# A transformer block on one core: one down tile moved from the attention loop into the tail's norm, wider spacing of one chunk's gate and up blocks, transposed tiles copied ahead of due work, and a reordered prologue

## The chip, the cores and the metric

The kernel runs on one core of a Trainium2 chip. A core has a matrix engine (TensorE, PE in the profile, with PEld for its weight loads), a vector engine (VectorE, DVE), a scalar engine that evaluates functions (ScalarE, ACT), a general engine (GpSimd, POOL) and a queue that issues transfers (SyncE, SP). Each works through its own list of instructions in order and waits on semaphores for the others. TensorE writes to PSUM; the other data is in SBUF. The metric is device time in microseconds, the median of several runs.

## The reference: what is computed

One transformer block, pre-norm, for 2048 rows of 512 features in bf16: 32 attention heads of 16 features, then a gated feed-forward layer of width 1792.

```python
def _A_ref(x, wqkv, wo):                      # S=2048, D=512, H=32, Dh=16
    qkv = (x @ wqkv).reshape(B, S, 3, H, Dh).transpose(2, 0, 3, 1, 4)
    q, k, v = qkv[0], qkv[1], qkv[2]
    scores = jnp.einsum("bhqd,bhkd->bhqk", q, k) * (Dh ** -0.5)
    p = _softmax(scores, axis=-1)
    o = jnp.einsum("bhqk,bhkd->bhqd", p, v)
    return o.transpose(0, 2, 1, 3).reshape(B, S, D) @ wo

def _B_ref(x, w_gate, w_up, w_down):          # F=1792
    g = jnp.einsum("bsd,df->bsf", x, w_gate)
    u = jnp.einsum("bsd,df->bsf", x, w_up)
    return jnp.einsum("bsf,fd->bsd", _sigmoid(g) * u, w_down)

h = x + _A_ref(_layernorm(x), wqkv, wo)
h2 = h + _B_ref(_layernorm(h), w_gate, w_up, w_down)
```

Inputs are normal times 0.05. The largest piece of work is 32 x 2048 x 2048 exponentials.

## The kernel before

**Prologue (L264 to L475).** Rows are loaded in tiles of 128. Per pair of tiles `u`, `stats(u)` computes mean and variance on VectorE (ScalarE for one pair), `apply(u)` normalizes, and `trans(u)` transposes on TensorE and copies the result to SBUF on ScalarE (L341). As soon as 512 rows are there, `k_mm(n)` computes their keys for the first heads, `square(n)` squares them for a bound on the scores, and `k_copy(n)` copies them to SBUF (L361) and issues a transfer that spreads them (`k_spread`, L221). `norm_part_of` and `norm_half` (L383, matmul L387) sum the squares, and `k_max` (L179) takes the maxima. From them comes the bound `bnd` (L466), which the scores need so that no exponential overflows. `v_prod` and `v_cast` make the values of tiles 0 and 1. At the end GpSimd copies one element of `bnd` (L472, which makes it wait for the bound) and then clears buffers (L473, L529, L1051). While the prologue runs, `pm_tile()` gives one of six PSUM tiles. `ps_misc` is a pool with a single PSUM tile, and `acc` another single one.

**The attention loop (L1057 to L1072).** The 2048 queries are cut into chunks 0, 1, 2 of 512 rows and chunks 3 and 4 of 256. A unit is one chunk, one group of four heads, one tile of keys and one head. Three units make a step; there are 683 steps. Step `i` writes its scores with TensorE into one of two PSUM buffers of three parts of 512 columns (L879), and ScalarE takes the exponential of all three (L890, 1.45 us). In every fourth step (`i % 4 == 0`, up to step 680, and some more in `twice`) the third part's exponential is left to VectorE as a polynomial: L909 reads PSUM at once, L912 and L915 follow one step later, L918 two, L922 three. The probabilities are multiplied with the values some steps later (`emit_pv`, L961, into `acc`), and at the end of a head group `emit_norm` copies `acc` (L935) and takes the row sums through DRAM and back to get their reciprocals (L938 to L950, on the SP queue); `scale` multiplies (L942) into `OT`.

**Fill work.** All other work of the loop is one generator, `filler`. It yields the cost of each matmul, and `emit_fill(i)`, called once per step, takes as much from it as `rate(i)` allows. A yield of `("at", n)` makes it wait for the next step whose number modulo 4 is `n` (its phase), `("gap", n)` for some steps, and `("from", n)` for step `n`. In the loop `pm_tile()` gives the one tile of `ps_misc`, so each piece of fill work waits until the one before it has been read out of PSUM.

**Order inside a step.** A step emits, in this order: scores, exponential, PV, what is due at this step (`due`: polynomial pieces, reciprocals, scalings, normalizations put there by `later`), and the fill work. Only in a step in which a head group's first PV unit falls is the fill emitted ahead of that unit. Since each engine works in order, this is also the order on VectorE.

**Feed-forward of a finished chunk (`ffn_tasks(c)`).** For each 128-row tile, `ffn_wo` (chunks 0, 1) or `ffn_wo_tight` (chunks 2, 3) runs eight projection matmuls (L598), adds x and normalizes (`wo_ln`, L607 and the norm's lines, the normalization itself two steps later), and then `hn_transpose` transposes (L162) and copies (L163). `ffn_up` runs gate blocks and up blocks alternately: eight matmuls of 256 columns or four of 512 (L622), the gate followed by a tanh on ScalarE (L627), the up block by a product on VectorE (L635). `ffn_down` runs 14 matmuls per tile (L638) and adds the residual (L643). Chunk 3's feed-forward runs during chunk 4's attention, and `wo_early` begins chunk 4's projection.

**Tail (`ffn_last`).** After the last exponential chunk 4's two tiles are finished alone: projection, statistics (L785, L795), normalized tile 0 on ScalarE (L798) and tile 1 on VectorE (L800), transposes (L791), copies (L792), gate and up, down (L823), output. `spin` issues matmuls whose result nobody reads (L253): six while the norm is computed, two after each transpose.

Of the kernel before, what the change touches and what calls it, by code (L numbers as in the profile page):

```python
# [19 lines left out]
def kernel(  # L20
# [243 lines left out]
    def prologue(pro):  # L264
# [156 lines left out]
        norm_part_of(0)  # L421
        k_chunk(1)
        stats(6)
        apply(5)
        trans(5)
        norm_mm_to(acc[:], sqs["q"])
        v0 = v_prod(0, pm_tile())
# [30 lines left out]
        half_copy(1)  # L458
        k_spread(ku, 0, slice(3 * QC, S), nc.sync)
        pn3 = ps_misc.tile([P, 512], FP32, name="pm")  # L460
        norm_half(pn3, 7)
        k_max(pn3[:, 0:QC // 2], km2[:, 2:3])
        v_cast(1, v_prod(1, ps_misc.tile([P, 512], FP32, name="pm")))
        m2 = k_most()
# [149 lines left out]

    def hn_transpose(tt, hn, copy=None):
        transpose4(hnT[:, :, tt * P:(tt + 1) * P], hn, copy)

# [29 lines left out]
    def ffn_wo(c):  # L647
        for tt, t in enumerate(tiles_of(c)):
            xr = x_load(t)
            yield ("at", 3)  # L650
            ps = pm_tile()
            for g in range(NG):
                if g == NG // 2:
                    yield ("at", 1)
                yield 1
                wo_mm(ps, c, tt, g)
            hn = wo_ln(ps, xr, tt)
            yield ("gap", 1)
            yield ("at", 1)
            yield 1  # L660
            hn_transpose(tt, hn)

    def ffn_wo_tight(c):
        turn = None
        for tt, t in enumerate(tiles_of(c)):
            xr = x_load(t)
            yield ("at", 3)
            ps = pm_tile()
            for g in range(NG):
                if g == NG // 2:  # L670
                    yield ("at", 0)
                yield 1
                wo_mm(ps, c, tt, g)
            hn = wo_ln(ps, xr, tt)
            if turn:
                yield ("at", 1)
                yield 1
                hn_transpose(*turn)
            turn = (tt, hn)
        yield ("gap", 1)  # L680
        yield ("at", 1)
        yield 1
        hn_transpose(*turn)

    def ffn_up(c):
        w = CHUNKS[c][1]
        at = cycle((3, 1) if c + 2 < NC else (3, 0, 1))
        for fs in blocks_of(w):
# [15 lines left out]
    def ffn_down(c, tight):  # L704
        at = 0
        for tt, t in enumerate(tiles_of(c)):
            for f in range(FC):
# [23 lines left out]
    def wo_early(c):  # L731
        early["x"] = [x_load(t) for t in tiles_of(c)]
        early[0] = pm_tile()
        for g in range(NG - 1):
            if g == NG - 2:
                yield ("from", NS - 4)
            yield 1
            wo_mm(early[0], c, 0, g)

    def ffn_last(c):  # L740
# [35 lines left out]
        for tt in range(n):  # L776
            wo(tt, NG - 1, NG)
        spin(acc, wo_pad[:, 0, :], 6)
        mv = small.tile([P, n, nc.vector.BN_AGGR_DIM], FP32, name="mvl")
# [25 lines left out]
        for tt in range(n):  # L805
            nc.vector.tensor_copy(out=h_sb[:, tt, :], in_=pss[tt][:])
        for fs in blocks_of(w):
# [10 lines left out]
        for tt, t in enumerate(ts):  # L818
            for cols in ((0, D),) if tt < n - 1 else ((0, D // 2), (D // 2, D)):
                cs = slice(*cols)  # L820
                psd = pm_tile()
                for f in range(FC):
                    nc.tensor.matmul(psd[:, cs], lhsT=hT[:, f, tt * P:(tt + 1) * P], rhs=wd[:, f, cs],  # L823
                                     start=(f == 0), stop=(f == FC - 1))
                ob = pmh["work"].tile([P, D], BF16, name="ob", tag="xn")
                nc.vector.scalar_tensor_tensor(out=ob[:, cs], in0=psd[:, cs], scalar=0.5, in1=h_sb[:, tt, cs],
                                               op0=ALU.mult, op1=ALU.add)
# [145 lines left out]
    fl = filler()  # L973
    state = {"wait": 0, "debt": 0.0, "done": False, "next": 0, "rate": None}

# [63 lines left out]
    with tc.manual_schedule():  # L1039
# [17 lines left out]
        for i in range(NS + LAG):  # L1057
# [7 lines left out]
            for u in us:  # L1065
                if early_fill and u[2] == 0:
                    emit_fill(i)
                emit_pv(*u[:3], i)
            for fn in due.pop(i, []):
                fn()  # L1070
# [39 lines left out]
```

## Time and profile before

| what | value |
|---|---|
| median of 3 runs | 959.14 us (958.26 to 960.2) |
| the profiled execution's own time | 958.45 us |
| its span, first to last instruction | 956.6 us |
| ScalarE busy | 898.2 us, 94% of the span |
| TensorE busy | 839.0 us, 88% |
| VectorE busy | 783.3 us, 82% |
| GpSimd busy | 40.0 us, 4% |
| first exponential starts, last one ends | 29.82 us, 926.60 us |
| granted TensorE clock | 1.0 of full speed |

The profile is one execution. Busy is the time in which an engine works on at least one instruction; shares are averages over stages with different limits. A row of the timeline gives the start, the duration, engine, line, operation, output<-inputs, the count of merged instructions, and in brackets how long the engine had been idle and what released it. A row of the waits gives who waited for whom, the microseconds in total, how many times, and the longest. TensorE's matmuls overlap: one of 512 columns takes about 0.38 us from start to end, but several together take less than their sum. Spans on GpSimd are rough.

### The profile page before, as it was taken

Reading aid. Unit: us, or ns where it says so; the run is one execution under the profiler, and the core shown is the slowest. Engines: PE = TensorE matmul, PEld = TensorE weight load, DVE = VectorE, ACT = ScalarE, POOL = GpSimd, SP = SyncE. Lnnn points to the kernel's source line nnn. Section 1 sums busy time; section 2 is a strip of 40 time slices with the busy share of each in tenths; the row PEclk is TensorE's granted clock in tenths of the full one; section 3 lists DMA queues with packets and bytes.
Section 4 is the critical chain, followed back from the end, with each engine's and each line's share of the span. In section 5 each row is a group of like instructions: output and inputs, shape, how many; then the busy total and the mean of one; then the engine's idle time right before and its main releaser. Section 6 shows DMA issues by size and latency. Waiting matters only on the chain.

```text
span 956.6 us, 17273 instructions
## 1 busy us (share of the span) xinstructions
PE 839.0 (88%) x6433; PEld 336.9 (35%) x6433; DVE 783.3 (82%) x1413; ACT 898.2 (94%) x778; POOL 40.0 (4%) x56
## 2 busy tenths in 40 slices
PE   5998888888788999998788999988788999998998
PEld 3322222222222322222222323222355555455656
DVE  7589988888788888899888888898898788777653
ACT  6889999999999999999999999999998999999872
POOL 5600000000000000000000000000000000000000
PEclk9999999999999999999999999999999999999999
DMA  5102350000003000000010000000010000110010
GB/s 161 24 2 56 115 117 16 16 16 14 16 14 103 15 16 17 20 24 23 4 26 27 16 17 16 19 9 27 16 31 23 17 10 15 27 32 16 10 35 12
DMA packets 37645, 28.45 MB, mean 30 GB/s; under 512 B 17788, under 2 KB 32920, under 8 KB 37560
## 3 DMA queue, kind: packets, MB, share of 16 engines
q1 hardware_dynamic: 37416, 27.22, 10.8%
q8 instruction: 50, 0.82, 0.4%
q14 instruction: 35, 0.29, 0.1%
q10 hardware_dynamic: 144, 0.13, 0.0%
HBM read 20.31 MB, written 2.61 MB: 24 GB/s over the span
## 4 chain that ended last, share of the span: by engine, by line
PE 45%; ACT 24%; DVE 22%; issue 6%; DMA 2%; SPq 1%; POOL 0%; ACTq 0%; DVEq 0%
PE pss L879 21%; ACT pt L890 13%; PE acc L961 8%; PE pm L622 7%; ACT stg L890 4%; ACT wd L890 4%; DVE stg L909 2%; PE pm L638 2%; ACT QTu L890 2%; PE pm L598 2%; PE pm L171 2%; DVE y L918 2%; DVE pt L922 2%; DVE reg L912 1%; DVE reg L635 1%
## 5 line engine op out<-in xcount | busy, mean ns | idle before, releaser
L879 PE MATMUL pss<-QB,KT 128*128 128x512 bf16 (+3 forms) x2554 | 476.0, 337 | 80.7 <-ACT pt L890 40.2
L890 ACT ACTIVATE pt<-pss 128x1536 bf16<-128x1536 f32 (+1 forms) x392 | 502.2, 1366 | 14.0 <-PE pss L879 9.5
L879 PEld LDWEIGHTS <-KT 64*128 64x128 bf16 (+1 forms) x2554 | 179.3, 95 | 340.5 <-issue 232.8
L890 ACT ACTIVATE stg<-pss 128x1536 bf16<-128x1536 f32 (+1 forms) x140 | 183.4, 1361 | 5.0 <-PE pss L879 3.8
L909 DVE TENSOR_SCALAR stg<-pss 128x512 int32<-128x512 f32 x123 | 84.8, 690 | 68.1 <-PE pss L879 59.9
L961 PE MATMUL acc<-pt,Vaug 128*17 128x512 bf16 (+1 forms) x1471 | 112.5, 338 | 2.3 <-DVE pt L922 1.1
L890 ACT ACTIVATE wd<-pss 128x1536 bf16<-128x1536 f32 (+1 forms) x80 | 103.9, 1391 | 1.9 <-PE pss L879 1.4
L890 ACT ACTIVATE QTu<-pss 128x1024 bf16<-128x1024 f32 (+1 forms) x71 | 95.9, 1350 | 1.7 <-PE pss L879 1.3
L915 DVE SCALAR_TENSOR_TENSOR y<-reg 128x512 f32<-128x512 f32 x123 | 85.2, 692 | 4.2
L918 DVE SCALAR_TENSOR_TENSOR y<-y,reg 128x512 f32<-128x512 f32 x123 | 84.3, 685 | 1.1
L961 PEld LDWEIGHTS <-Vaug 128*17 128x17 bf16 x2560 | 49.2, 89 | 94.7 <-issue 80.3
L622 PE MATMUL pm<-reg,reg 128*128 128x512 bf16 (+1 forms) x280 | 57.9, 337 | 7.9 <-DVE reg L635 7.6
L622 PE MATMUL pm<-reg,wu 128*128 128x512 bf16 (+1 forms) x280 | 58.1, 338 | 1.4 <-ACT sg L627 1.1
L638 PE MATMUL pm<-wd,reg 128*128 128x512 bf16 x196 | 55.6, 382 | 1.9 <-DVE ob L643 1.9
L912 DVE TENSOR_SCALAR reg<-stg 128x512 int32<-128x512 int32 x123 | 52.0, 422 | 1.8
L961 PE MATMUL acc<-stg,Vaug 128*17 128x256 bf16 (+1 forms) x564 | 50.6, 326 | 0.3 <-DVE stg L922 0.2
L635 DVE SCALAR_TENSOR_TENSOR reg<-sg,pm 128x512 bf16<-128x512 f32 x56 | 38.2, 683 | 14.2 <-PE pm L622 13.8
L922 DVE SCALAR_TENSOR_TENSOR pt<-y,stg 128x512 bf16<-128x512 f32 x70 | 48.0, 686 | 2.0
L152 POOL TENSOR_TENSOR rs<-ve,pw_neg 128x1 f32<-128x1 f32 x16 | 11.8, 735 | 877.1 <-DVE ve L150 870.5
L627 ACT ACTIVATE sg<-pm 128x512 f32<-128x512 f32 x56 | 36.5, 651 | 10.4 <-PE pm L622 9.9
L909 DVE TENSOR_SCALAR wd<-pss 128x512 int32<-128x512 f32 x45 | 31.0, 689 | 17.9 <-PE pss L879 16.5
L171 PE MATMUL pm<-reg 128*128 128x512 bf16 x124 | 38.3, 398 | 1.8 <-DVE stg L526 0.7
(151 smaller groups left out, 715.8 us busy)
## 6 DMA issues: line engine op xcount, KB each, us to landing
rb_all<-rd SPq DMA_DIRECT2D x96, 64.0 KB
xr<-in_A_x_dram SPq DMA_DIRECT2D x16, 128.0 KB
out_dram<-ob SPq DMA_DIRECT2D x15, 128.0 KB
rb_all<-rd SPq DMA_DIRECT2D x60, 32.0 KB
reg<-in_A_x_dram SPq DMA_DIRECT2D x7, 256.0 KB
KT<-stg SPq DMA_DIRECT2D x7, 256.0 KB
reg<-in_B_w_gate_dram SPq DMA_DIRECT2D x4, 448.0 KB
wu<-in_B_w_up_dram SPq DMA_DIRECT2D x4, 448.0 KB
```

Of the source, the lines that this page charges most:

```text
L171: nc.tensor.matmul(ps[:], lhsT=wqkv_sb[:, c, w0:w0 + P], rhs=xnT[:, c, n * QC:(n + 1) * QC], start=(c == 0), stop=(c == DC - 1))
L622: nc.tensor.matmul(ps[:, i * w:(i + 1) * w], lhsT=wt[:, c, f * P:(f + 1) * P], rhs=hnT[:, c, 0:w], start=(c == 0), stop=(c == DC - 1))
L635: nc.vector.scalar_tensor_tensor(out=out, in0=a, scalar=1.0, in1=b, op0=ALU.add, op1=ALU.mult)
L638: nc.tensor.matmul(ps[:], lhsT=hT[:, f, tt * P:(tt + 1) * P], rhs=wd[:, f, :], start=(f == 0), stop=(f == FC - 1))
L879: nc.tensor.matmul(pss[:, ui, h * w:(h + 1) * w], lhsT=KT[rows, g, kt * P:(kt + 1) * P], rhs=QB[n_qg % 2][rows, j, 0:w], start=True, stop= ...
L890: ex = nc.scalar.activation(out=pt[:, 0:na, :], in_=pss[:, 0:na, :], func=ACT.Exp, scale=DH ** -0.5 / QS)
L909: return nc.vector.tensor_scalar(out=e_bits, in0=src, scalar1=ONE_BITS, scalar2=0.0, op0=ALU.add, op1=ALU.max)
L912: nc.vector.tensor_scalar(out=e_man, in0=e_bits, scalar1=0x7FFFFF, scalar2=-0x40800000, op0=ALU.bitwise_and, op1=ALU.bitwise_or)
L915: nc.vector.scalar_tensor_tensor(out=e_pol, in0=m, scalar=PA, in1=m, op0=ALU.add, op1=ALU.mult)
L918: nc.vector.scalar_tensor_tensor(out=e_pol, in0=e_pol, scalar=PB, in1=e_man.bitcast(FP32), op0=ALU.add, op1=ALU.mult)
L922: nc.vector.scalar_tensor_tensor(out=dst, in0=e_pol, scalar=PC, in1=e_bits.bitcast(FP32), op0=ALU.add, op1=ALU.mult)
L961: nc.tensor.matmul(acc[32 * j:32 * j + VW, 0:w], lhsT=Vaug[:, kt, 4 * g + j, :], rhs=p[:, h * w:(h + 1) * w], start=(kt == 0), stop=(kt == ...
```

## The change

- `ffn_down(3)` leaves out its last tile. `ffn_last` runs that tile's 14 matmuls in place of the six `spin` matmuls in the norm, and its `down_out` after the copies of the two residual tiles. Those copies go to slots `n + tt` of `h_sb`, since the left-out tile's residual is still in slot 1.
- `ffn_up(3)` places its blocks at phases 3, 1, 3, 0, 1 in turn; before, at 3, 0, 1.
- `wo_early` holds its last matmul (group 6) behind the loop by three yields instead of one.
- A flag `state["turn"]` is set before a tile's transposes. In the step in which the fill may go on, the fill is then emitted ahead of what is due, so that the copy of the transposed tile stands on VectorE ahead of the polynomial pieces and scalings of that step. `hn_transpose` clears the flag.
- In the prologue the copy of key chunk 1 (`k_copy(1)`) is issued after `trans(5)`. The value product of tile 1 goes into `acc`, two of its matmuls ahead of `norm_half(7)` and two behind it; before, it used the single tile of `ps_misc` after `k_max` had released it.

```diff
@@ prologue
-        k_chunk(1)
+        ps1 = k_mm(1)
+        square(1, ps1[:])
         stats(6)
         apply(5)
         trans(5)
+        k_copy(1, ps1)
         norm_mm_to(acc[:], sqs["q"])
...
+        for c in range(2):
+            v_mm(acc, 1, c)
         pn3 = ps_misc.tile([P, 512], FP32, name="pm")
         norm_half(pn3, 7)
         k_max(pn3[:, 0:QC // 2], km2[:, 2:3])
-        v_cast(1, v_prod(1, ps_misc.tile([P, 512], FP32, name="pm")))
+        for c in range(2, DC):
+            v_mm(acc, 1, c)
+        v_cast(1, acc)
@@ hn_transpose
+        state["turn"] = False
         transpose4(hnT[:, :, tt * P:(tt + 1) * P], hn, copy)
@@ ffn_wo, and the same before the transposes in ffn_wo_tight
             yield ("gap", 1)
+            state["turn"] = True
             yield ("at", 1)
@@ ffn_up
-        at = cycle((3, 1) if c + 2 < NC else (3, 0, 1))
+        at = cycle((3, 1) if c + 2 < NC else (3, 1, 3, 0, 1))
@@ ffn_down
-        for tt, t in enumerate(tiles_of(c)):
+        for tt, t in enumerate(tiles_of(c)[:None if c < NC - 2 else -1]):
@@ wo_early
             if g == NG - 2:
-                yield ("from", NS - 4)
+                for _ in range(3):
+                    yield ("from", NS + LAG)
@@ ffn_last
-        spin(acc, wo_pad[:, 0, :], 6)
+        psd = pm_tile()
+        for f in range(FC):
+            down_mm(psd, f, len(tiles_of(c - 1)) - 1)
...
         for tt in range(n):
-            nc.vector.tensor_copy(out=h_sb[:, tt, :], in_=pss[tt][:])
+            nc.vector.tensor_copy(out=h_sb[:, n + tt, :], in_=pss[tt][:])
+        down_out(psd, tiles_of(c - 1)[-1], len(tiles_of(c - 1)) - 1)
...
-                nc.vector.scalar_tensor_tensor(out=ob[:, cs], in0=psd[:, cs], scalar=0.5, in1=h_sb[:, tt, cs],
+                nc.vector.scalar_tensor_tensor(out=ob[:, cs], in0=psd[:, cs], scalar=0.5, in1=h_sb[:, n + tt, cs],
@@ the loop, between a step's PV and its due work
+            if state["turn"] and i == state["wait"] and not early_fill:
+                emit_fill(i)
+                early_fill = True
             for fn in due.pop(i, []):
                 fn()
```

## The prediction

> **What bounds the kernel now.** I read the busy times first, then ScalarE's waits stretch by stretch, then the chain and the timeline where those waits are long.
>
> ```profile
> PE 839.0 (88%) x6433; PEld 336.9 (35%) x6433; DVE 783.3 (82%) x1413; ACT 898.2 (94%) x778; POOL 40.0 (4%) x56
> ```
>
> ScalarE (ACT) is busy 94% of the span. From the first exponential (L890, 29.82 us) to the end of the last (926.60 us) it goes from step to step almost without a hole, and its work in that stretch is not changed. So the loop gets shorter by the ScalarE idle time that goes, the start by the time at which the first exponentials can run, and the end by the chain behind the last one. ScalarE's waits from 870 to 930 us (chunk 3's gate, up and down work), then from 733 to 800 us (chunk 2's gate and up work):
>
> ```profile
> ACT pt L890 <- PE pss L879: 2.1, 5, 0.8
> ACT stg L890 <- PE pss L879: 1.5, 4, 0.8
> ACT QTu L890 <- PE pss L879: 0.8, 1, 0.8
> ACT sg L627 <- PE pm L622: 0.4, 1, 0.4
> ...
> ACT stg L890 <- PE pss L879: 0.3, 1, 0.3
> ACT sg L627 <- PE pm L622: 0.2, 1, 0.2
> ```
>
> Here 4.8 us are lost in 60, there 0.5 us in 67. Chunk 2 puts its blocks two steps apart (phases 3, 1), chunk 3 at phases 3, 0, 1, so that two of three follow in adjacent steps. The timeline shows what that does: an up block cannot start before the tanh (L627) has read the one shared PSUM tile, the next scores stand behind the block, and the exponential starts 0.81 us late.
>
> ```profile
> 900.06 0.59 ACT L627 ACTIVATE sg<-pm 128x512 f32<-128x512 f32 x1
> 900.70 1.03 PE L622 MATMUL pm<-reg,wu 128*128 128x256 bf16 x8 [0.45 <-ACT sg L627]
> 902.37 5.29 ACT L890 ACTIVATE pt<-pss 128x1536 bf16<-128x1536 f32 x4 [0.81 <-PE pss L879]
> ```
>
> In chunk 2's norm a transposed tile's copy (L163) stands on VectorE behind the polynomial exponential (L912, L915) and holds the PSUM tile that the next output-projection matmuls want:
>
> ```profile
> 722.59 0.42 DVE L163 COPY reg<-pm 128x512 bf16<-128x512 bf16 x1
> 723.06 1.02 PE L598 MATMUL pm<-wo_pad,OT 128*128 128x512 bf16 x4 [1.01 <-DVE reg L163]
> 725.49 1.02 ACT L890 ACTIVATE pt<-pss 128x1024 bf16<-128x1024 f32 x1 [1.42 <-PE pss L879]
> ```
>
> In the tail's norm TensorE runs six filler matmuls and then waits for the normalized tile:
>
> ```profile
> 930.69 1.46 PE L253 MATMUL acc<-wo_pad,ident_bf 128*128 128x512 bf16 x6
> 933.66 0.40 PE L791 MATMUL pm<-ident_bf,xn 128*128 128x128 bf16 x4 [1.51 <-ACT xn L798]
> ```
>
> And in the prologue:
>
> ```profile
> 20.33 0.62 ACT L361 CAST stg<-pm 128x512 bf16<-128x512 f32 x1
> 21.92 1.02 PE L171 MATMUL pm<-reg 128*128 128x512 bf16 x4 [0.39 <-ACT reg L341]
> 27.38 1.02 PE L166 MATMUL pm<-reg 128*128 128x512 bf16 x4 [0.52 <-DVE km L179]
> 40.62 3.54 POOL L529 MEMSET KT<- 128x2048 bf16 x2
> 43.13 1.31 DVE L912 TENSOR_SCALAR reg<-wd 128x512 int32<-128x512 int32 x1
> ```
>
> **The change, part by part.**
>
> *Blocks of chunk 3 wider, one down tile out of the loop.* Seven gate and seven up blocks, first at step 647. Now they stand at 647, 648, 649, 651 and so on, the last at 664: nine neighbours in adjacent steps. Afterwards they stand at 647, 649, 651, 652, 653, 655, 657, 659, 660, 661, 663, 665, 667, 668: five. The idle time by kind, from ScalarE's holes now: gate then up across phases 3 to 0 is 0.81, 0.81, 0.81; gate then up across 0 to 1 is 0.38, 0.38; up then gate across 3 to 0 is 0.33, 0.35; up then gate across 0 to 1 is 0.43 and 0. Sum 4.30 us. The five that remain are two of the first kind (1.62), one of the second (0.38), one of the third (0.34), one of the fourth (0.21, the mean): 2.55 us. The eight now separated cost what chunk 2's do, 0.5 us in 27 blocks, so 0.15. The down work has holes of 0.13, 0.17, 0.48 and 0.17 (0.95 us) in ten stops; 0.48 is the second tile waiting for the first one's result (L643). Five stops (steps 671 to 676) remain: 0.30. Together 5.25 now, 3.00 after: **-2.25 us**. The ends: -0.65 if the block waits only move, -5.25 if all holes close.
>
> *The tail.* Fourteen matmuls of 512 columns take the place of six fillers. The final down work gives their pitch: 14 of 512 and 28 of 256 columns in 6.24 us is 0.223 each. From 930.69 to the transposes at 933.66 there are 2.97 us; 14 need 3.1. The first transposes slip about 0.1 us, but the second ones (934.38) wait for the other normalized tile, and the gate blocks for its copy: **+0.05 us**, ends 0 and +3.7 (0.379 for one alone and 0.097 for its weight load, as the rows of that final down work, L823, have them, with nothing overlapped: 6.7). The new result (L643, 0.69 us) follows the two copies that end at 936.44 on VectorE, so it ends at 937.13; the first product (L635) starts at 937.33: covered by the two blocks that TensorE runs until then. Should that cover go, 0.7 us at most. Its output transfer has over fifteen microseconds to the end.
>
> *Last projection matmuls.* Group 6 of the early tile stays behind the last PV matmuls as now, at nothing: 926.79 is set by the last exponential. On SP the kept tile's output and two x loads (0.42 and 0.93 us of issue) now come ahead of the last reciprocal's transfers. That reciprocal (921.04) waits 1.65 us for sums whose issue started at 919.39, and the three issues fit into that; the output that stands ahead of those sums now (0.45 us) is gone. The scaled group is ready at 926.33 and wanted at 927.12: 0.8 us of cover, at nothing; 1 us if it is used up.
>
> *Copies ahead of what falls due.* Fourteen copies, each ahead of L912 and L915 (1.1 us) and, in some steps, the scaling (L942). Only two were waited for: 1.01 and 0.18 us. The long one: the copy could run at 721.18 instead of 722.59, the projection matmuls at 722.05, but the sixteen PV matmuls behind them want the accumulator's copy (L935), which still ends at 723.33. They start at 723.38, not 724.01: 0.63. With 0.18 for the other, **-0.8 us**; ends -1.2 and 0. The price: VectorE stands still until the transposes are done. By their ends against the preceding instruction's end that is about 0.3 us at three tiles and under 0.1 at two, in stages where ScalarE has no hole: nothing. Behind each waiting copy stand L912 and L915, with PV five steps off.
>
> *Prologue order.* K copy 1 (L361) moves behind the transposed tile's copy (L341). The chain runs through both, 0.48 us of it in L361. TensorE could start chunk 2's K at 21.46: 0.45 us for all that follows. K copy 1's own transfer waits on SP anyway, behind eight query issues that end at 23.64. The value product of tile 1 in `acc` lets two matmuls run before the norm (L387) and spares the wait of 0.52; its copy also leaves before the first exponential. The bounds (L466) would be ready at 27.77, the first exponential at 28.77: 1.05 us earlier. But GpSimd's nine memsets start with the bounds and move by 0.45 only, their last from 42.37 to 41.92, its end from 44.16 to 43.71. L912, 0.42 us elsewhere, took 1.31 beside it and ended 0.28 after it. From there VectorE runs without a hole to the value copy that releases TensorE at 47.88, and the exponential at 49.53. So what arrives is **-0.45 us**; ends 0 and -1.05.
>
> The SBUF — State Buffer page of the Trainium skill, section "Who interferes with whom", has the rule behind that row: VectorE in a two-port mode and GpSimd share a port pair, whoever issues first holds it for its whole instruction, and the other blocks. By it L912, coming at 42.1, waits for the memset that started at 41.9: -0.45; without it -1.05 would stand.
>
> **Sum:** -2.25 + 0.05 - 0.8 - 0.45 = -3.45 us against the profiled execution's 958.45 (span 956.6 and 1.85 around it): 955.0. The median of the runs is 959.14, 0.69 above the profiled one, so I forecast 955.7 for it.
>
> **The rivals.**
> - *GpSimd's memset is not in the way.* L912 would come only some 0.15 us after the memset's start, and GpSimd's spans are rough; a little earlier, and it slips in. Then -1.05 in place of -0.45: 955.1.
> - *The block waits only move.* TensorE's other work per step stays, and a hole closed at one step may open at the next. For it: step 657's up-then-gate has no hole, step 649's has 0.43, so the kinds are not constant. Against: three holes of 0.81 within 2 ns. Then -0.65 in place of -2.25: 957.3.
> - *The copies win nothing*, because PV or the next norm sets step 540: 956.5.
> - *Slower: the tail's down tile is not covered.* If its matmuls and weight loads do not overlap, +3.7, and the time is 959.3 (with the copies' gain gone too it would be over 960). It decides from 3.5 us over the hole, 0.46 us a matmul. Against it stands the pitch of 0.223 in the same tail.
>
> **How the numbers follow.** What a measurement here can tell from no change is about 0.2%, 1.9 us. Chances: the forecast 0.50, the memset out of the way 0.12, block waits that move 0.18, copies that win nothing 0.10, the uncovered tail and anything else that ends slower 0.10. The first, second and fourth are faster by over 0.2%, apart from their edges and the spread of the runs (958.26 to 960.2); the third sits on the border. Faster 0.68, within 0.2% 0.21, slower 0.11. The range goes from the memset rival with the copies' full 1.2 (954.7) and half a microsecond of spread, 954.2, to the moved waits with the copies winning nothing and the same spread, 958.6. The forecast's own: 954.7 to 957.
>
> **What would show it.** ScalarE's waits between the first gate block and the last exponential near 3 us, with two holes of 0.81; no wait of TensorE on L163 at chunk 2's second tile; first exponential near 28.8, the fourteenth only near 49.1; in the tail fourteen L638 matmuls and transposes within 0.2 us of now, counted from the last exponential. Wrong if holes appear between the spaced blocks, if L791 waits for L638, or if VectorE's stops for the transposes reach ScalarE.

## The result, and the profile after

The first measurement of the changed kernel has a median of 953.45 us (952.48 to 953.62), against 958.70 us for the kernel before beside it: ratio 0.9943, 95% interval 0.9925 to 0.9961. It is faster by about 0.6%. The direction was forecast, but the time lies below the range (954.2 to 958.6), and two more measurements later gave medians of 954.27, just inside the range, and 953.71. The profiled execution took 953.62 us with a span of 951.8; its last exponential ends at 921.87 us (926.60 before) and 29.97 us follow it (30.03 before).

I call the n-th exponential, counted from 0, *step* n (also index n), and compare its start in both profiles. L904 is the exponential now (L890 before), L893 the scores, L629 and L634 the blocks and the tanh, L645 the down matmuls.

| stretch | change of its length, us | the prediction's term |
|---|---|---|
| up to step 13 | -0.65 | prologue -0.45 |
| steps 36 to 40 | +1.22 | none |
| steps 40 to 50 | -0.44 | none |
| steps 50 to 530 | +0.42 | none |
| steps 530 to 545 | -0.86 | copies ahead -0.8 |
| steps 545 to 647 | -0.23 | none |
| steps 647 to 682 (chunk 3) | -4.21 | blocks and down tile -2.25 |
| behind the last exponential | -0.06 | tail +0.05 |

The sum is -4.81, as the spans have it; -3.45 was forecast. The first view is the profile's busy times, then ScalarE's waits over chunk 3 (865 to 925 us) and over chunk 2 (733 to 800 us) of the changed kernel.

```profile
PE 838.9 (88%) x6427; PEld 336.7 (35%) x6427; DVE 783.8 (82%) x1413; ACT 897.1 (94%) x778; POOL 39.4 (4%) x56
```

```profile
...
ACT stg L904 <- PE pss L893: 1.6, 3, 0.8
ACT pt L904 <- PE pss L893: 0.8, 1, 0.8
...
ACT sg L634 <- PE pm L629: 0.2, 1, 0.2
```

No engine does noticeably less; ScalarE's 4.8 us of named waits in chunk 3 are now 2.4, in four places. The timeline around chunk 2's second tile and around one of the four holes:

```profile
721.51 0.41 DVE L163 COPY reg<-pm 128x512 bf16<-128x512 bf16 x1
721.60 1.45 ACT L904 ACTIVATE QTu<-pss 128x1536 bf16<-128x1536 f32 x1
722.18 0.42 DVE L926 TENSOR_SCALAR reg<-stg 128x512 int32<-128x512 int32 x1
722.36 1.04 PE L604 MATMUL pm<-wo_pad,OT 128*128 128x512 bf16 x4
722.94 1.45 ACT L904 ACTIVATE pt<-pss 128x1536 bf16<-128x1536 f32 x1
725.18 1.02 ACT L904 ACTIVATE pt<-pss 128x1024 bf16<-128x1024 f32 x1 [0.80 <-PE pss L893]
...
879.75 1.45 ACT L904 ACTIVATE pt<-pss 128x1536 bf16<-128x1536 f32 x1 [0.81 <-PE pss L893]
```

L163 runs ahead of L926 (a piece of the polynomial exponential, L912 before) and the projection (L604) no longer waits for it; the exponential behind it has a hole of 0.80 where it had 1.42. Step 540 comes 0.63 us sooner behind the step before it than in the old kernel, and step 536 0.24; the prediction had 0.63 and 0.18. The rows of 721.60 and 722.94 also show what I had missed: the second exponential starts 1.34 us after the first, although each lasts 1.45. The start of one overlaps the end of the other by about 0.11. The row at 879.75 starts behind a hole and has no such overlap.

The tail and the prologue of the changed kernel:

```profile
40.02 3.54 POOL L535 MEMSET KT<- 128x2048 bf16 x2
41.91 1.93 DVE L926 TENSOR_SCALAR reg<-wd 128x512 int32<-128x512 int32 x1
...
925.89 3.19 PE L645 MATMUL pm<-wd,reg 128*128 128x512 bf16 x14
928.91 0.39 PE L804 MATMUL pm<-ident_bf,xn 128*128 128x128 bf16 x4
```

The fourteen down matmuls fill the norm's wait, and the transposes start 7.04 us behind the last exponential (7.06 before). In the prologue L926 at step 8 lasts 1.93 us where it lasted 1.31: it comes earlier and still ends only behind GpSimd's memset, which started at 40.02 us where it started at 40.62.

The surprise is at steps 36 to 40. The table of windows of the changed kernel (length; busy time of PE, PEld, DVE, ACT, POOL; PEclk; DMA share; GB/s) and its timeline:

```profile
79.00:82.00 3.00, 1.83 (x9) 0.54 (x9) 2.93 (x6) 3.00 (x4) 0.00 (x0) 0.96 0.10 25
82.00:85.00 3.00, 3.00 (x17) 0.39 (x15) 2.90 (x6) 2.57 (x3) 0.00 (x0) 0.50 0.36 109
```

```profile
81.17 0.61 PE L893 MATMUL pss<-QB,KT 64*128 64x512 bf16 x3 [0.75 <-ACT pt L904]
81.70 1.03 PE L171 MATMUL pm<-reg 128*128 128x512 bf16 x2
82.67 1.03 PE L893 MATMUL pss<-QB,KT 64*128 64x512 bf16 x3
```

From 81.7 us, for 3.41 us, TensorE's granted clock is half: three score matmuls take 1.03 in place of 0.61, and two exponentials wait. It cost 1.2 us. The profile of before has no such window. Executions of both kernels hit none, one or several of them, so below I give the median of all executions and also the mean of those at granted clock 1.0. Before: 958.63 (the 86 executions beside the experiments) and 957.48 (27 at 1.0). After: 953.70 (20) and 953.04 (8 at 1.0), so that at equal clock the change is worth 4.4 us. Two executions far from all others, 2668.20 us of the kernel before and 3548.82 us of the spacing undone, are left out of these means.

### The profile page after: what moved, and what is told of

The parts are those of the page before. It is cut to its first block, busy times and chain, and to the rows that moved or that the text cites. A ratio compares the mean times of both kernels' runs of the same rounds, so it can differ in the third digit from the quotient of the medians.

```text
span 951.8 us, 17268 instructions
## 1 busy us (share of the span) xinstructions
PE 838.9 (88%) x6427; PEld 336.7 (35%) x6427; DVE 783.8 (82%) x1413; ACT 897.1 (94%) x778; POOL 39.4 (4%) x56
## 4 chain that ended last, share of the span: by engine, by line
PE 45%; ACT 24%; DVE 23%; issue 6%; DMA 1%; SPq 1%; POOL 0%; ACTq 0%; DVEq 0%
PE pss L893 22%; ACT pt L904 13%; PE acc L975 8%; PE pm L629 6%; ACT stg L904 4%; ACT wd L904 4%; DVE stg L923 3%; ACT QTu L904 2%; PE pm L645 2%; DVE pt L936 2%; PE pm L171 2%; DVE y L932 2%; DVE reg L926 1%; PE pm L604 1%; DVE y L929 1%
## 5 line engine op out<-in xcount | busy, mean ns | idle before, releaser
L893 PE MATMUL pss<-QB,KT 128*128 128x512 bf16 (+3 forms) x2554 | 476.7, 337 | 80.9 <-ACT pt L904 40.7
L904 ACT ACTIVATE pt<-pss 128x1536 bf16<-128x1536 f32 (+1 forms) x392 | 502.2, 1367 | 12.9 <-PE pss L893 7.7
L893 PEld LDWEIGHTS <-KT 64*128 64x128 bf16 (+1 forms) x2554 | 179.7, 95 | 341.4 <-issue 235.1
L904 ACT ACTIVATE stg<-pss 128x1536 bf16<-128x1536 f32 (+1 forms) x140 | 183.3, 1360 | 4.7 <-PE pss L893 3.1
L904 ACT ACTIVATE wd<-pss 128x1536 bf16<-128x1536 f32 (+1 forms) x80 | 103.8, 1390 | 3.0 <-PE pss L893 2.8
L904 ACT ACTIVATE QTu<-pss 128x1024 bf16<-128x1024 f32 (+1 forms) x71 | 95.9, 1350 | 0.9 <-PE pss L893 0.5
L629 PE MATMUL pm<-reg,reg 128*128 128x512 bf16 (+1 forms) x280 | 58.0, 338 | 6.3 <-DVE reg L642 5.9
L629 PE MATMUL pm<-reg,wu 128*128 128x512 bf16 (+1 forms) x280 | 58.1, 338 | 1.2 <-ACT sg L634 1.2
L645 PE MATMUL pm<-wd,reg 128*128 128x512 bf16 x196 | 54.9, 382 | 1.3 <-DVE ob L650 1.3
L926 DVE TENSOR_SCALAR reg<-stg 128x512 int32<-128x512 int32 x123 | 51.8, 421 | 1.5
L634 ACT ACTIVATE sg<-pm 128x512 f32<-128x512 f32 x56 | 36.7, 654 | 9.7 <-PE pm L629 9.6
```

Of the source, the lines that this page charges most:

```text
L629: nc.tensor.matmul(ps[:, i * w:(i + 1) * w], lhsT=wt[:, c, f * P:(f + 1) * P], rhs=hnT[:, c, 0:w], start=(c == 0), stop=(c == DC - 1))
L645: nc.tensor.matmul(ps[:], lhsT=hT[:, f, tt * P:(tt + 1) * P], rhs=wd[:, f, :], start=(f == 0), stop=(f == FC - 1))
L893: nc.tensor.matmul(pss[:, ui, h * w:(h + 1) * w], lhsT=KT[rows, g, kt * P:(kt + 1) * P], rhs=QB[n_qg % 2][rows, j, 0:w], start=True, stop= ...
L904: ex = nc.scalar.activation(out=pt[:, 0:na, :], in_=pss[:, 0:na, :], func=ACT.Exp, scale=DH ** -0.5 / QS)
L926: nc.vector.tensor_scalar(out=e_man, in0=e_bits, scalar1=0x7FFFFF, scalar2=-0x40800000, op0=ALU.bitwise_and, op1=ALU.bitwise_or)
```

## The experiments

Ratios are to the kernel before, measured beside it. Diffs are against the changed kernel unless said otherwise.

**The spacing undone.**

```diff
-        at = cycle((3, 1) if c + 2 < NC else (3, 1, 3, 0, 1))
+        at = cycle((3, 1) if c + 2 < NC else (3, 0, 1))
```

> The changed kernel with chunk 3's gate and up blocks back at phases 3, 0, 1; its last down tile stays in the tail's norm. Theory A (the spacing closes the holes, and each closed hole gives back its idle time plus some 0.13 us of overlap that the next exponential had lost): the steps 647 to 682, which took 54.36 us before and 50.15 after, take 52.9 to 53.1 us, and the time is about 2.8 us above the changed kernel's, some 956.3. Rival B (taking the down tile out of the loop relieved TensorE, and the spacing does little): the steps take less than 51.2 us and the time is within 1 us of the changed kernel's.

Median 959.20 us, ratio 1.000 (0.9986 to 1.0014); at clock 1.0 956.83 (two executions), 3.8 above the changed kernel. Steps 647 to 682 take 54.23 us, more than theory A's 53.1, so theory A holds in kind and is too small in size. ScalarE's waits there (870 to 926 us) are back:

```profile
ACT pt L904 <- PE pss L893: 1.6, 4, 0.8
ACT stg L904 <- PE pss L893: 1.4, 3, 0.8
ACT QTu L904 <- PE pss L893: 1.2, 2, 0.8
ACT sg L634 <- PE pm L629: 0.5, 1, 0.5
```

Rival B falls: with the tile out and the old spacing, 0.13 of 4.21 us is left in these steps. Next to their idle time the holes carry what the overlap would have saved: an exponential behind a hole comes 0.11 to 0.14 us later than the hole explains, one before which both a tanh and an exponential had holes 0.24. Measured from start to start (1.330 us a full exponential, 0.904 a short one, 0.477 more with a tanh), steps 647 to 682 lost 7.88 us before: 5.24 visible and 2.64 hidden. Now they lose 3.67: 2.43 and 1.24. There were 15 holes and are four; eleven times 0.12 is 1.3 of the 1.40 by which the hidden part fell. Not all of the hidden part belongs to holes: the last version below, which has none in these steps, still loses 0.69 by this measure.

**The spacing alone**, in the kernel before:

```diff
-        at = cycle((3, 1) if c + 2 < NC else (3, 0, 1))
+        at = cycle((3, 1) if c + 2 < NC else (3, 1, 3, 0, 1))
```

> The kernel before with one edit: chunk 3's gate and up blocks at phases 3, 1, 3, 0, 1; both of its down tiles stay in the loop. Theory A (the spacing is what closes the holes, and the down tile's move to the tail only makes room for the stops of the later blocks): the steps 647 to 682, 54.36 us before, take about 51.3 (50.15 and about 1.1 for the second tile's stops), the tail behind the last exponential stays at 30.0, and the time is about 3 us below the kernel before. Rival B (without the tile's move there is no room in the loop): what does not fit runs behind the last exponential, the tail grows by over 1.5 us, and the time is less than 1.5 us below the kernel before.

Median 957.02, ratio 0.9988 (0.9978 to 0.9997); at clock 1.0 955.43, 2.05 below before. Each theory has half: the steps take 50.80 us, a gain of 3.56, but the tail takes 31.56 and gives 1.53 back. The timeline behind the last steps:

```profile
923.27 0.38 PE L638 MATMUL pm<-wd,reg 128*128 128x512 bf16 x1 [0.16 <-issue]
924.43 2.10 PE L598 MATMUL pm<-wo_pad,OT 128*128 128x512 bf16 x9 [0.44 <-DVE ob L643]
```

The last down matmul runs at 923.27, level with the last exponential's end (923.56), and nine projection matmuls come behind it. So the spacing earns most of the time in the loop, and the tile's move saves the tail from paying for it; with the spacing in place the move also takes 0.65 out of the steps (50.80 to 50.15).

**Copies behind what falls due again.**

```diff
-            if state["turn"] and i == state["wait"] and not early_fill:
-                emit_fill(i)
-                early_fill = True
```

> The changed kernel with the copies of transposed tiles behind what falls due again. Theory A (the long wait of chunk 2's second tile was worth what it cost at the exponential): TensorE waits about 1.0 us on that copy again, the steps 530 to 545 take about 21.85 us in place of 20.98, and the time is 0.9 to 1.3 us above the changed kernel's, some 954.5. Rival B (what follows has slack by now, or the PV matmuls behind set the exponential): those steps stay within 0.2 us of 20.98, or a later hole closes, and the time is within 0.3 us.

Median 954.98, ratio 0.9969 (0.9954 to 0.9984); at clock 1.0 954.16, 1.1 above the changed kernel. Steps 530 to 545 take 21.84. Theory A holds in place and size.

**The prologue's order of before.** (The edit takes the prologue's lines of the diff back.)

> The changed kernel with the prologue's order of before. Theory A (0.65 us is what arrives behind GpSimd's last memset, and the half-clock window of TensorE at 82 to 85 us has another cause): first exponential at 29.8 us, the fourteenth (index 13) at 49.5 in place of 48.9, and the time 0.65 us above the changed kernel's, some 954.1. Rival B (the new order of the prologue brings the half-clock window): its granted clock is 1.0 in every run, the steps 36 to 40 lose no 1.2 us, and the time is 953.5 or less.

Median 955.07, ratio 0.9962 (0.9945 to 0.9979); 2 of 10 executions at clock 1.0, at 952.66. Both theories miss. Rival B falls, since eight of the ten executions are below clock 1.0. The first exponential is at 29.25 us and not 29.8, index 13 at 48.96 and not 49.5, although the code is that of before. What differs is the moment at which TensorE's clock came full: 16.0 us of the span here, 17.8 in the profile of before. The profile of the spacing alone has the same prologue and lies between (17.3 us; 29.60 and 49.31). In the new order the moment makes no such difference: in its fifteen profiles it lies between 14.5 and 17.7 us, and the first exponential between 28.59 and 28.69. So against an execution with a late full clock the new order is worth 1.2 us at the first exponential and 0.6 at index 13, and against this one 0.65 and 0.07.

At step 50 it is 0.44 (98.64 against 98.20 in a profile of the new order without a half-clock window). Behind that the gain is given back. Steps 201, 507 and 628 start 0.90, 1.07 and 1.41 us behind the step before them in the three profiles with the old order, and 1.15, 1.34 and 1.68 or 0.02 more in the fifteen with the new one. Step 530 starts at 709.50 here, and between 709.49 and 709.72 in three profiles of the new order without a half-clock window up to there. So the +0.42 from step 50 to 530 comes with the prologue's order too. What makes these steps longer stays open; in the profile after, a transfer of an instruction queue (q14 on the page) starts some 0.7 us behind the start of each (287.8, 682.1 and 846.4 us), which proves no cause. At the end of the kernel the new order can't be told from nothing.

**GpSimd's memset out of the way.**

```diff
-            later(60 + g4, lambda g4=g4: nc.gpsimd.memset(wo_pad[:, g4:g4 + 4, :], 0.0))
+            later(60 + g4, lambda g4=g4: nc.vector.memset(wo_pad[:, g4:g4 + 4, :], 0.0))
```

> The changed kernel with the two clears of the padded output weights (steps 60 and 64) on VectorE instead of GpSimd. Theory A (VectorE's polynomial of step 8 is held up by GpSimd's last memset, so what that memset's place sets is all that the earlier start is worth): without the two clears GpSimd ends some 3.5 us earlier, the first polynomial instruction of step 8 takes 0.42 us in place of 1.93, the exponential of index 13 runs at about 48.3 in place of 48.9, and the time is 0.5 to 0.6 us below the changed kernel's, some 952.9. Rival B (VectorE's own queue of copies sets that exponential): the instruction takes 0.42, but the exponential of index 13 stays at 48.9 and the time within 0.2 us.

```profile
41.91 0.42 DVE L926 TENSOR_SCALAR reg<-wd 128x512 int32<-128x512 int32 x1
```

L926, at the same time, lasts 0.42 instead of 1.93, and index 13 is at 48.32: GpSimd's memset was the cause. By the Trainium skill (SBUF — State Buffer, "Who interferes with whom") VectorE in a two-port mode and GpSimd exclude each other, and the one that issues later is held for the other's whole instruction; the two rows agree. The time did not follow: median 955.18, ratio 0.9960 (0.9946 to 0.9975), 953.05 at clock 1.0. The two clears take 0.91 us each on VectorE, and the steps from 50 to 200 became 0.9 longer (187.45 against 186.55).

**The same in eight small pieces.**

```diff
-        for g4 in (0, 4):
-            later(60 + g4, lambda g4=g4: nc.gpsimd.memset(wo_pad[:, g4:g4 + 4, :], 0.0))
+        for g in range(NG):
+            later(56 + 2 * g, lambda g=g: nc.vector.memset(wo_pad[:, g, :], 0.0))
```

> The changed kernel with the clears of the padded output weights on VectorE in eight pieces, at steps 56, 58 and so on to 70, in place of two pieces on GpSimd. Theory A (GpSimd's memsets hold up VectorE at step 8 and that is worth 0.57 us, which two clears of 0.91 us on VectorE gave back with 0.9 at the exponentials; pieces of about 0.25 us fit between VectorE's other work): index 13 at 48.3 us, step 200 at or below 0.4 us under the changed kernel's 284.75 without a half-clock window, and runs at clock 1.0 about 0.5 us below the changed kernel's. Rival B (VectorE has no slack at all in these steps): step 200 is not earlier, and the time is not below the changed kernel's.

Median 952.54, ratio 0.9948 (0.9931 to 0.9965); 952.36 at clock 1.0, 0.7 below the changed kernel. Index 13 is at 48.34, step 200 at 284.26. Theory A holds.

**The half-clock windows.** First the changed kernel once more, then with two fillers at 22 steps, then at two.

```diff
+        for _ in range(2 if i in QUIET else 0):
+            nc.tensor.matmul(pss[:, 0, :], lhsT=ident_bf[:], rhs=KT[:, group[0][1], 0:QC], start=True, stop=True)
```

> The changed kernel as it is, run again for more executions beside the next three. Theory A (TensorE's half-clock windows follow a stretch of 3.41 us in which TensorE was busy for less than about 0.62 of it, and the order of the work has a dozen such stretches, so that each execution hits none, one or a few of them by the place at which its clock came full): the runs spread from 952.5 to about 956, about one in three at granted clock 1.0 and those near 952.9, each 0.002 of granted clock costing about 1.2 us; the median near 953.8. Rival B (the two runs with a half-clock window seen so far were chance, and it is gone in most): median within 0.4 us of 952.9.

Median 954.27, ratio 0.9966 (0.9950 to 0.9981), 952.77 to 959.17; 3 of 10 at clock 1.0 (953.12), four at 0.998 (954.30), one each at 0.996 (956.09), 0.995 (956.87) and 0.993 (959.17). Theory A holds; by rival B the median would lie within 0.4 of 952.9.

> The changed kernel with two filler matmuls of 512 columns ahead of the scores at 22 steps, which lie in the eleven stretches of 3.41 us in which TensorE was busy for less than 0.62 of the time (around 78, 199, 209, 243, 258, 263, 484, 525, 622, 700 and 848 us). Theory A (low activity in a window brings the half-clock window that follows): no half-clock window ahead of the last exponential in the profile, granted clock 1.0 in at least 8 of 10 runs, and the median 953.0 or less, with a much smaller spread; the fillers themselves fit into waits of TensorE and cost under 0.3 us. Rival B (the half-clock windows have nothing to do with what TensorE does): as many runs below clock 1.0 as in the changed kernel, and the median as there or later.

Eight of ten executions are at clock 1.0, as theory A said (three of ten in the changed kernel beside it), which speaks against rival B. Its other numbers fail: the profile has one half-clock window, at 754.9 us behind a new stall, and the fillers cost far more than 0.3: 957.89 at clock 1.0, 4.9 above the changed kernel (median 958.20, ratio 0.9997, 0.9987 to 1.0007). Where TensorE's own order is on the path, each pair delayed its exponential by 0.2 to 0.3. The new stall is once more a scaling on VectorE that waits 2.13 us for its transfer.

> The changed kernel with two filler matmuls of 512 columns ahead of the scores of steps 35 and 36 alone. Theory A (the half-clock window at 82 to 85 us follows TensorE's emptiest stretch of the loop, 0.49 busy from 77.8 to 81.2 us): no half-clock window between 78 and 90 us in the profile, the fillers cost 0.1 us or nothing there, and more than 3 of 10 runs are at granted clock 1.0, by 2 or so. Rival B (the emptiness has no part in it): a half-clock window near 82 us in the profile if the clock came full between 16.3 and 17.0 us, as in the changed kernel.

Inconclusive. The clock came full at 14.5 us, so that the rival's condition wasn't met, and only 2 of 10 executions are at clock 1.0 (median 956.45, ratio 0.9976, 0.9962 to 0.9991). These two are 1.7 above the changed kernel's, though the fillers cost 0.06 at step 36. Its profile shows where that comes from: 1.0 at step 592 (3.04 us behind the step before it, 2.04 in the profile after), where VectorE stands 2.08 us at a scaling (L958 here) whose transfer has not landed, and 1.4 in the tail, with the same wait:

```profile
923.50 0.43 DVE L958 TENSOR_TENSOR OT<-xs_all,rb_all 128x256 bf16<-128x256 f32 x1 [6.05 <-DMA rb_all<-rd]
924.21 0.59 PE L604 MATMUL pm<-wo_pad,OT 128*128 128x512 bf16 x2 [1.77 <-DVE OT L958]
```

**All blocks two steps apart**, `at = cycle((3, 1))`.

> The changed kernel with chunk 3's gate and up blocks two steps apart throughout (phases 3, 1, as in chunk 2), the last at step 674 in place of 668. Theory A (only neighbours in adjacent steps make the holes that are left): the steps 647 to 682 take 47.0 to 48.0 us in place of 50.15, and the time is 2 to 3 us below the changed kernel's. Rival B (the down tile's stops and the last projection have no room behind step 674): new holes between steps 674 and 682 or a tail longer by over 1 us, and a time within 1 us of the changed kernel's or above it.

Median 953.36, ratio 0.9955 (0.9938 to 0.9972); 952.10 at clock 1.0, 1.0 below the changed kernel beside it. The steps take 49.12 us, over theory A's 48.0, and the gain is half of the 2 us that it said: the four holes are gone and one stall is new, 1.66 us of idle time in two pieces. It lies at steps 655 and 656 and not behind 674, where rival B had it; the tail is 30.67. The timeline there:

```profile
880.02 0.42 DVE L956 TENSOR_TENSOR OT<-xs_all,rb_all 128x256 bf16<-128x256 f32 x1 [2.26 <-DMA rb_all<-rd]
881.42 0.68 DVE L642 SCALAR_TENSOR_TENSOR reg<-sg,pm 128x512 bf16<-128x512 f32 x1
882.15 1.03 PE L629 MATMUL pm<-reg,reg 128*128 128x256 bf16 x8 [1.92 <-DVE reg L642]
883.22 0.60 ACT L634 ACTIVATE sg<-pm 128x512 f32<-128x512 f32 x1 [1.11 <-PE pm L629]
884.37 1.02 ACT L904 ACTIVATE stg<-pss 128x1024 bf16<-128x1024 f32 x1 [0.55 <-PE pss L893]
```

Read downwards: the scaling of a finished group waits on VectorE for its transfer; the block's product stands behind it, the next block behind that, and then the tanh and the exponential. A scaling is due a fixed number of steps after its sums, and here these steps, with the holes gone, are over before the transfer has landed.

**Seven widths in place of five**, `(3, 1, 3, 1, 3, 0, 1)`.

> The changed kernel with chunk 3's gate and up blocks at phases 3, 1, 3, 1, 3, 0, 1: three neighbours in adjacent steps, the last block at step 671. Theory A (each pair of neighbours costs its hole and about 0.13 us of lost overlap, and the down tile has room behind step 671): three of the four holes of the changed kernel stay, the steps 647 to 682 take 49.0 to 49.6 us in place of 50.15, and runs at granted clock 1.0 lie 0.5 to 1.0 us below the changed kernel's. Rival B (a hole opens elsewhere, as the 0.55 us at step 656 did with all blocks two steps apart): 50.0 or more, and no gain.

The steps take 49.85 us, outside both forecasts; clock 1.0 gives 952.81 (median 956.29, ratio 0.9970, 0.9956 to 0.9983). Six holes remain, of 0.11 to 0.55 us, the longest at step 656; theory A had three.

**Spacing, two fillers and small clears together.**

> The changed kernel with all three: chunk 3's blocks two steps apart (phases 3, 1), the fillers at steps 35 and 36, and the clears in eight pieces on VectorE. Theory A (the three gains are in different stages and add up): 1.0 from the spacing, about 0.5 from the clears and fewer half-clock windows, runs at clock 1.0 near 951.5 and a median about 2 us below the changed kernel's, some 952.2. Rival B (what is gained early is lost where VectorE or a later stage sets the pace): median 953 or above.

Median 953.11, ratio 0.9944 (0.9922 to 0.9965), of four executions; the one at clock 1.0 took 950.26. Steps 647 to 682 take 48.31. The median is where rival B had it, and the one execution at clock 1.0 is below theory A's 951.5, so this decides nothing.

**The x loads behind the last reciprocal's transfers**, beside the changed kernel again.

```diff
-        early["x"] = [x_load(t) for t in tiles_of(c)]
...
-        xrs = early["x"]
+        xrs = [x_load(t) for t in ts]
```

> The changed kernel as it is, beside the next three on the same chip. In the tail the scaled last group is ready between 0.1 us before and 1.8 us after TensorE wants it; runs at granted clock 1.0 near 953.0.

> The changed kernel with the two x loads of the last chunk behind the last reciprocal's transfers on SP instead of ahead of them. Theory A (the x loads' 256 KB slow the small transfers behind them): from the reciprocal to the scaled group 4.9 us as in the kernel before, in place of 5.5 to 6.9, the scaled group ready before the last exponential ends, TensorE's wait for it gone, the tail 29.9 us or less, and runs at clock 1.0 about 0.3 us below the changed kernel's. Rival B (the chain has a fixed latency and the closed holes alone moved the last exponential towards it): the reciprocal itself comes no earlier, and the chain takes 5.5 us or more all the same; no gain.

The changed kernel first, then the edit, in the tail:

```profile
924.94 0.42 DVE L956 TENSOR_TENSOR OT<-xs_all,rb_all 128x256 bf16<-128x256 f32 x1 [5.08 <-DMA rb_all<-rd]
925.42 0.82 PE L604 MATMUL pm<-wo_pad,OT 128*128 128x512 bf16 x3 [0.69 <-DVE OT L956]
```

```profile
924.08 0.42 DVE L955 TENSOR_TENSOR OT<-xs_all,rb_all 128x256 bf16<-128x256 f32 x1 [4.09 <-DMA rb_all<-rd]
924.84 0.82 PE L604 MATMUL pm<-wo_pad,OT 128*128 128x512 bf16 x3
```

From the reciprocal (919.11 and 919.23) to the scaling it takes 5.83 us in the changed kernel and 4.85 with the loads behind. TensorE's wait of 0.69 is gone, and the tail is 30.10 in place of 30.52. At clock 1.0 952.38 (two executions) against 953.07 (three); the medians, 954.00 and 953.71, don't show a gain (ratios 0.9940, 0.9922 to 0.9959, and 0.9949, 0.9933 to 0.9965). Theory A holds for the chain, not quite for the tail (29.9 or less). The other profiles bear it out: with the loads ahead, in eleven, the chain takes 5.36 to 6.85 us, and in the six where they come behind and nothing else holds the scaling up, 4.85 to 5.13.

**Spacing, small clears and x loads; then the scaling one step later.** The diff is that of the second against the first.

```diff
-            later(i + 10 + wait, scale)
+            later(i + 10 + wait + (c == NC - 1 and g < NG - 2), scale)
```

> The changed kernel with chunk 3's blocks two steps apart, the clears in eight pieces on VectorE and the x loads behind the last reciprocal's transfers. The gains of the three are in different stages: 1.0, 0.6 and some 0.3 us. Runs at clock 1.0 near 951.2. A hole of 0.9 to 1.7 us at the steps 655 and 656 stays, where VectorE's queue stands before a scaling (L956 in the changed kernel) that waits for its transfer.

> The previous kernel with the scaling of the last chunk's early groups one step later. Theory A (with the holes closed the scaling falls due before its transfer has landed, and the up block's product queued behind it on VectorE is late): the hole at the steps 655 and 656 falls below 0.4 us, the steps 647 to 682 take 47.0 to 47.6 us, and runs at clock 1.0 lie about 1 us below the previous kernel's, near 950.2. Rival B (the hole is TensorE's or the block's own): it stays, and the time too.

The first has a median of 953.90 (ratio 0.9945, 0.9925 to 0.9965), with 951.83 for its one execution at clock 1.0. Its profile loses 2.29 us at step 655, in part to a half-clock window that follows the stall at 883.70 us; all blocks two steps apart, without such a window, lost 1.91 there. With the scaling one step later it does not wait,

```profile
878.70 0.42 DVE L955 TENSOR_TENSOR OT<-xs_all,rb_all 128x256 bf16<-128x256 f32 x1
```

ScalarE has no wait at all from 865 to 917 us, and the steps take 47.17 us. Median 949.72 us (949.28 to 950.99), ratio 0.9908 (0.9890 to 0.9927); 949.57 at clock 1.0 (three of four executions). Theory A holds, with 2.3 us at clock 1.0 where it said about 1. This version is faster than the kernel before by 9.4 us in the median and 7.6 at clock 1.0, and than the changed kernel by 4.0 and 3.5.

## Why the prediction was wrong

- **Blocks and down tile, -2.25: this step failed, by size.** The mechanism is as told: one shared tile, adjacent blocks, holes of 0.81. The term was mis-sized in "Together 5.25 now, 3.00 after". It priced a hole by ScalarE's idle time from one end to the next start. But exponentials in a row overlap, by 0.12 (1.45 long, 1.330 apart), and one behind a hole does not. That hidden part went from 2.64 to 1.24, which is -1.40 that no wait in the profile names. The visible part went from 5.24 to 2.43, -2.81: four holes remained and not five, and the separated blocks and the down stops, for which 0.45 was kept, had none. The sum of both is the measured -4.21. The Trainium skill (ScalarE: Activation LUTs, "What ACT_TABLE_LOAD costs") states that back-to-back ACTIVATEs overlap by about 93 ns; the trace has 0.12. The tile's share was kept at 0.65 (0.95 less 0.30). It is that with the spacing in place (50.80 against 50.15) and 0.13 without (54.36 against 54.23), so the two gains are not a plain sum. That the spacing needs the move, since the tail is 1.5 us longer without it, was not in the prediction.
- **Tail +0.05: right in the first profile** (-0.06). Fourteen matmuls took 3.19 us, 3.1 forecast. The changed kernel's two later profiles have tails of 30.07 and 30.52, for the reason that follows.
- **Last projection at nothing: right in the first profile, but not safe.** The 0.8 us of cover is used up. In that profile the scaled group is ready at 922.37 and wanted at 922.31; in eight others TensorE waits 0.45 to 1.77. I had counted the x loads on SP as issue time only. With them ahead the chain of small transfers takes 1.0 us longer (5.83 against 4.85).
- **Copies ahead -0.8: right** (-0.86 in these steps, 1.1 on the whole time when undone).
- **Prologue -0.45: near where it was read, nothing at the end.** The mechanism holds against the profile of before: the memsets start with the bounds, and both came 0.60 earlier (the last memset from 42.37 to 41.77), the memset holds L926, and index 13 moved by 0.65. The rival without the memset falls; with it away index 13 comes another 0.57 earlier. Two things were not in the term. Of the 0.60, 0.57 goes when the old order meets an early full clock. And the step "so what arrives" fails: by step 530 the old order has caught up.
- **Not in the sum:** the half-clock window, +1.22 in the profiled execution, and the stretch from step 50 to 530, +0.42, which comes with the prologue's order and whose cause stays open. The -0.23 from step 545 to 647 is mostly the wait ahead of step 592, which differs between profiles (1.81 to 3.04 us behind the step before it in the 18). Without the half-clock window the profiled time would have been about 952.4, further still below the range.
- **The rivals.** Block waits that only move: no, the waits went. Copies that win nothing: no, 0.86. The uncovered tail: no, fourteen matmuls took 3.19 us and not 6.7.

## What to carry to other kernels

Price a hole on a saturated engine from start to start against its own back-to-back pitch, not by the idle time that the profile names: each hole here cost 0.11 to 0.14 us more than that. Where holes are closed ahead of work that is due after a fixed number of steps, look for the transfer behind it, for the steps get shorter and the transfer doesn't; having the last chunk's early scalings one step later was worth some 2 us. An early gain is worth what is left of it at the end: the prologue's was gone by step 530. And compare two profiles only after looking at when the clock came full and whether it was halved in between.

## What the runs showed of the hardware

- **Half-clock windows in mid-kernel.** I cut each of the 18 profiles into windows of 3.413 us from the moment at which the clock came full, and took TensorE's busy share in each. All sixteen half-clock spells begin at a boundary of these windows, and each follows a window with a busy share of at most 0.622. Of the 55 windows below 0.625 that the loop and tail have, 16 were followed by one; of the 4787 above, none. The two kernels have a dozen places in the loop whose emptiest 3.4 us lie below 0.62, and where the cut falls differs between executions. One window costs 1.2 us or a little more (957.48, 958.74 and 960.07 for the kernel before at clock 1.0, 0.998 and 0.996). The Trainium skill (TensorE: Matmul & The Clock Gate, "What's actually happening") has the free-running window of 3413 ns, and the trace agrees. It asks for an idle window ahead of the half clock; here a window busy for 0.38 to 0.62 of the time was enough at times. What tells the 16 from the other 39 stays open.
- **The start of the full clock** lies between 14.5 and 17.8 us of the span. In the old prologue the first exponential followed it (full at 16.0, 17.3 and 17.8 us; exponential at 29.25, 29.60 and 29.82); in the new order it stayed within 0.1 us (28.59 to 28.69).
- **Small transfers behind two loads of 128 KB** took 1.0 us longer from reciprocal to scaling (5.83 against 4.85, in two profiles with the same half-clock windows).
